# An attention output projection whose two operands are widened to float32r by casting DMAs

## The chip, the cores and the metric

The kernel runs on one core of a Trainium2 chip. The time is device microseconds of one execution; the median of 2 runs is shown. The profile is one execution, taken by the hardware profiler, and its times are microseconds from the first instruction.

## The reference

Two blocks follow each other on x of 2048 positions by 1024 features, in bfloat16. The first is a layer norm, a projection to q, k and v, a local attention of 32 heads of 32 features, and an output projection with `wo`. The second is a layer norm and a gated feed-forward network without an activation function.

```python
def attn(x, wqkv, wo):            # x: 2048 x 1024, H = 32 heads, Dh = 32
    q, k, v = split(x @ wqkv)
    # each position sees W = 8 keys, at distances 0, 2, 4 ... 14 behind it
    logits = einsum("bhsd,bhswd->bhsw", q, kg) * Dh ** -0.5   # masked before the start
    o = einsum("bhsw,bhswd->bhsd", softmax(logits), vg)
    return o @ wo                 # wo: 1024 x 1024
def ffn(x, w_gate, w_up, w_down): # F = 3584
    return ((x @ w_gate) * (x @ w_up)) @ w_down
h = x + attn(layernorm(x), wqkv, wo)
out = h + ffn(layernorm(h), w_gate, w_up, w_down)
```

## The kernel before

The 2048 positions are cut into four chunks of 512. For each chunk the work has these stages, all named by functions in the code.

- `ln1` loads x, normalises it on VectorE (DVE) and transposes it on TensorE (PE, line 111); ScalarE (ACT) copies the result to `lnT`.
- `qkv` multiplies by six blocks of `wqkv` of 512 columns each (`wq`, lines 134 and 144). All six are loaded once and stay for the four chunks. ACT copies each result out of PSUM to a tile `sg`, and SP writes it to tensors `qd`, `kd`, `vd` in device memory.
- `attention` reads these back in another layout, `qD`, `kD`, `vD`, by DMAs on the queue of POOL (GpSimd). There each of 128 partitions holds one head of one quarter of the chunk. Its arithmetic runs on DVE: products and sums for the logits (lines 177 to 183), softmax, then products and sums with v (lines 208 to 214) into `oD`. POOL writes `oD` to `od` in device memory, and reads it back by four DMAs as `oT` (line 218), the transposed layout that a matmul needs.
- `wo_ln2` is the output projection: two halves of 512 columns, and in each four tiles of 128 positions with 8 matmuls of 128x512 (line 234). DVE adds each result to x in `hs` (line 236). Then follow the second layer norm and its transposes.
- `ffn1` runs 7 blocks of gate and up weights (`wg`, `wu`, lines 251 and 255); ACT copies out of PSUM and DVE multiplies the two (line 261, `gs`).
- `ffn2` multiplies by `w_down` (line 290, in the last half of the last chunk line 277); DVE adds to `hs` (line 293), and SP stores the output.

Three things set the order. Each engine and each DMA queue runs its instructions in the order in which a scheduler placed them, after the priorities given by `prio`; the attention of the next chunk has a later place than the feed-forward work of the present chunk on PE, but runs beside it on DVE. Every wait is for data or for a buffer. And buffers come from pools: `wstream` has 6 buffers of 8 KB a partition, through which all weights go in turn, wqkv's six blocks first. `att` has one buffer for each tag, so a tile with the same tag as an earlier one waits until the last reader of that is done. PSUM has 6 buffers for matmul results (`mm`) and 2 for transposes; `t1k` has 31 buffers for `sg`, `gs` and `us`.

The projection of chunk 0 stands on PE between the two halves of `qkv` of chunk 3, that of a later chunk between `ffn1` and `ffn2` of the chunk before it.

Of the kernel before, what the change touches and what calls it, by code (L numbers as in the profile page):

```python
# [7 lines left out]

BF = mybir.dt.bfloat16
F32 = mybir.dt.float32  # L10
ALU = mybir.AluOpType
ACTF = mybir.ActivationFunctionType
PSUM = bass.MemoryType.PSUM
# [5 lines left out]
DH = 32  # L19
# [7 lines left out]
SUB = TC // 4  # L27
KO = D // 128
# [8 lines left out]
def kernel(  # L37
# [11 lines left out]
    nc = tc.nc  # L49
# [12 lines left out]
    wpool = ctx.enter_context(tc.tile_pool(name="wstream", bufs=6))  # L62
# [6 lines left out]
    att = ctx.enter_context(tc.tile_pool(name="att", bufs=1))  # L69
# [6 lines left out]
    make_identity(nc, ident[:])  # L76
    eps = const.tile([128, 1], F32)
    nc.vector.memset(eps[:], EPS)
    mask = const.tile([32, W, 16], F32)
    nc.vector.memset(mask[:], 0.0)  # L80
# [9 lines left out]
    wo_v = A_wo.rearrange("(kk p) n -> p kk n", p=128)  # L90
# [6 lines left out]
    def layernorm_T(src, dstT, col):  # L97
        st = small.tile([128, 2, nc.vector.BN_STATS_DIM], F32, tag="st")
        for i in range(2):
            nc.vector.bn_stats(out=st[:, i, :], in_=src[:, bass.ts(i, 512)])  # L100
        mv = small.tile([128, nc.vector.BN_AGGR_DIM], F32, tag="mv")
        nc.vector.bn_aggr(out=mv[:], in_=st[:])  # L102
        lnv = small.tile([128, 1], F32, tag="lnv")
        nc.scalar.activation(lnv[:], mv[:, 1:2], ACTF.Ln, bias=eps[:])  # L104
        rstd = small.tile([128, 1], F32, tag="rstd")
        nc.scalar.activation(rstd[:], lnv[:], ACTF.Exp, scale=-0.5)
        ln = lnp.tile([128, D], BF, tag="ln")
        nc.vector.tensor_scalar(ln[:], src[:], mv[:, 0:1], rstd[:], ALU.subtract, ALU.mult)  # L108
        pt = pstp.tile([128, KO, 128], BF, tag="pt")
        for kk in range(KO):  # L110
            nc.tensor.transpose(pt[:, kk, :], ln[:, bass.ts(kk, 128)], ident[:])  # L111
        nc.scalar.copy(dstT[:, :, col:col + 128], pt[:])  # L112
# [47 lines left out]
    def attention(c):  # L160
        qD = att.tile([128, DH, SUB], BF, tag="qD")
        kD = att.tile([128, DH, SUB + HB], BF, tag="kD")
        vD = att.tile([128, DH, SUB + HB], BF, tag="vD")
        nc.gpsimd.dma_start(qD[:], qd[c].rearrange("c g d s -> (c g) d s"))
        for (tD, td) in ((kD, kd), (vD, vd)):
            if c == 0:
                nc.gpsimd.dma_start(td[c][0, :, :, 0:HB], zt[:])
            else:
                nc.gpsimd.dma_start(td[c][0, :, :, 0:HB], td[c - 1][3, :, :, SUB:SUB + HB])
            nc.gpsimd.dma_start(tD[:], td[c].rearrange("c g d s -> (c g) d s"))  # L170
        lg = att.tile([128, W, SUB], F32, tag="lg")
        for wp in range(W // 2):
            prod = att.tile([128, 2, DH, SUB], BF, tag="prod")
            for j in range(2):
                w = 2 * wp + j
                o = HB - DIL * w
                nc.vector.tensor_tensor(prod[:, j], qD[:], kD[:, :, o:o + SUB], ALU.mult)  # L177
            nc.vector.tensor_tensor(prod[:, :, 0:16], prod[:, :, 0:16], prod[:, :, 16:32], ALU.add)  # L178
            nc.vector.tensor_tensor(prod[:, :, 0:8], prod[:, :, 0:8], prod[:, :, 8:16], ALU.add)
            t3 = att.tile([128, 2, 4, SUB], F32, tag="t3")  # L180
            nc.vector.tensor_tensor(t3[:], prod[:, :, 0:4], prod[:, :, 4:8], ALU.add)
            nc.vector.tensor_tensor(t3[:, :, 0:2], t3[:, :, 0:2], t3[:, :, 2:4], ALU.add)
            nc.vector.tensor_tensor(lg[:, 2 * wp:2 * wp + 2, :], t3[:, :, 0], t3[:, :, 1], ALU.add)
        if c == 0:
            nc.vector.tensor_tensor(lg[0:32, :, 0:16], lg[0:32, :, 0:16], mask[:], ALU.add)
        tr = att.tile([128, 4, SUB], F32, tag="t3")
        nc.vector.tensor_tensor(tr[:], lg[:, 0:4], lg[:, 4:8], ALU.max)
        nc.vector.tensor_tensor(tr[:, 0:2], tr[:, 0:2], tr[:, 2:4], ALU.max)
        mx = att.tile([128, SUB], F32, tag="mx")
        nc.vector.tensor_tensor(mx[:], tr[:, 0], tr[:, 1], ALU.max)  # L190
        nc.vector.tensor_tensor(lg[:], lg[:], mx[:, None, :].to_broadcast((128, W, SUB)), ALU.subtract)
        nc.scalar.activation(lg[:], lg[:], ACTF.Exp, scale=float(DH) ** -0.5)
        tr2 = att.tile([128, 4, SUB], F32, tag="t3")
        nc.vector.tensor_tensor(tr2[:], lg[:, 0:4], lg[:, 4:8], ALU.add)
        nc.vector.tensor_tensor(tr2[:, 0:2], tr2[:, 0:2], tr2[:, 2:4], ALU.add)
        sm = att.tile([128, SUB], F32, tag="mx")
        nc.vector.tensor_tensor(sm[:], tr2[:, 0], tr2[:, 1], ALU.add)
        rs = att.tile([128, SUB], F32, tag="rs")
        nc.vector.reciprocal(rs[:], sm[:])
        at = att.tile([128, W, SUB], BF, tag="at")  # L200
        nc.vector.tensor_tensor(at[:], lg[:], rs[:, None, :].to_broadcast((128, W, SUB)), ALU.mult)
        oD = att.tile([128, DH, SUB], BF, tag="oD")
        for wp in range(W // 2):
            pv = att.tile([128, 2, DH, SUB], BF, tag="prod")
            for j in range(2):
                w = 2 * wp + j
                o = HB - DIL * w
                nc.vector.tensor_tensor(pv[:, j], vD[:, :, o:o + SUB],  # L208
                                        at[:, w, None, :].to_broadcast((128, DH, SUB)), ALU.mult)
            if wp == 0:  # L210
                nc.vector.tensor_tensor(oD[:], pv[:, 0], pv[:, 1], ALU.add)
            else:
                nc.vector.tensor_tensor(pv[:, 0], pv[:, 0], pv[:, 1], ALU.add)  # L213
                nc.vector.tensor_tensor(oD[:], oD[:], pv[:, 0], ALU.add)  # L214
        nc.gpsimd.dma_start(od[c].rearrange("c g d s -> (c g) d s"), oD[:])
        oT = att.tile([128, KO, 4, SUB], BF, tag="oT")
        for cp in range(4):
            nc.gpsimd.dma_start(oT[:, :, cp, :], od[c][cp].rearrange("(hg hl) d s -> (hl d) hg s", hl=4))
        return oT

    def wo_ln2(c, oT):
        lnT = lnTp.tile([128, KO, TC], BF, tag="lnT")
        hs = []
        for t in range(4):
            ht = hp.tile([128, D], BF, tag="h")
            nc.sync.dma_start(ht[:], x[bass.ds(c * TC + t * 128, 128), :])
            hs.append(ht)
        for hf in range(2):
            wt = wpool.tile([128, KO, 512], BF, tag="w")
            nc.sync.dma_start(wt[:], wo_v[:, :, bass.ts(hf, 512)])  # L230
            for t in range(4):
                ps = psmm.tile([128, 512], F32, tag="mm")
                for kk in range(KO):
                    nc.tensor.matmul(ps[:], lhsT=oT[:, kk, t, :], rhs=wt[:, kk, :],  # L234
                                     start=(kk == 0), stop=(kk == KO - 1))
                nc.vector.tensor_tensor(hs[t][:, bass.ts(hf, 512)], ps[:], hs[t][:, bass.ts(hf, 512)], ALU.add)  # L236
        for t in range(4):
            layernorm_T(hs[t], lnT, t * 128)
        return lnT, hs
# [60 lines left out]
    for b in range(6):  # L300
        with prio(-9900 + 1000 * (b // 2) + b):
            wt = wpool.tile([128, KO, 512], BF, tag="w", name=f"wq{b}")
            nc.sync.dma_start(wt[:], wqkv_v[:, :, bass.ts(b, 512)])
            wq_sb.append(wt)
    for c in range(NCH):
        qkv(c, lnTs[c], B0)
        if c + 1 < NCH:
            with prio(-10000 + 1000 * (c + 1)):
                lnTs[c + 1] = ln1(c + 1)
        else:  # L310
            with prio(1000000):
                oT = attention(0)
            nxt = wo_ln2(0, oT)
        qkv(c, lnTs[c], B1)
    for c in range(NCH):
        lnT2, hs = nxt
        hT = ffn1(c, lnT2)
        if c + 1 < NCH:
            with prio(1000000 + (c + 1) * 20000):
                oT = attention(c + 1)  # L320
            nxt = wo_ln2(c + 1, oT)
        ffn2(c, hT, hs)
# [30 lines left out]
```

## Time and profile before

| what | value |
|---|---|
| median of the runs | 855.4 us (854.95 to 855.85) |
| span of the profiled execution | 853.2 us |
| PE busy | 827.4 us (97%), 4000 matmuls |
| PE weight loads busy | 383.4 us (45%) |
| DVE busy | 465.1 us (55%) |
| ACT busy | 234.6 us (27%) |
| POOL busy | 29.9 us (4%) |
| DMA | 151.65 MB, mean 178 GB/s |

The span goes from the first to the last instruction; what lies around it, 2.2 us to the median, is not in the profile. The profiled execution has no other time of its own than this span. Busy times of PE are those of pipelined matmuls: their lengths overlap, so that the distance between starts says more than the length of one. Lines such as L234 are lines of the kernel. "PEld" is TensorE's loading of weights, "SPq" and "POOLq" are the engines' queues as they issue DMAs.

### The profile page before, as it was taken

Reading aid. Unit: us, or ns where it says so; the run is one execution under the profiler, and the core shown is the slowest. Engines: PE = TensorE matmul, PEld = TensorE weight load, DVE = VectorE, ACT = ScalarE, POOL = GpSimd, SP = SyncE. Lnnn points to the kernel's source line nnn. Section 1 sums busy time; section 2 is a strip of 40 time slices with the busy share of each in tenths; the row PEclk is TensorE's granted clock in tenths of the full one; section 3 lists DMA queues with packets and bytes.
Section 4 is the critical chain, followed back from the end, with each engine's and each line's share of the span. In section 5 each row is a group of like instructions: output and inputs, shape, how many; then the busy total and the mean of one; then the engine's idle time right before and its main releaser. Section 6 shows DMA issues by size and latency. Waiting matters only on the chain.

```text
span 853.2 us, 9977 instructions
## 1 busy us (share of the span) xinstructions
PE 827.4 (97%) x4000; PEld 383.4 (45%) x4000; DVE 465.1 (55%) x523; ACT 234.6 (27%) x421; POOL 29.9 (4%) x46
## 2 busy tenths in 40 slices
PE   5999999969999997999999999999999999999998
PEld 4544444434444443444444444444444444444443
DVE  6719999998999999999931421111116102111011
ACT  4744333305333312003333120133332003333200
POOL 1000000200020000100000010000000000000000
PEclk9999999989999999999999999999999999999999
DMA  9896646975676743956455465653625465353520
GB/s 311 247 262 167 173 99 176 233 265 148 173 240 210 250 157 132 284 160 214 154 191 177 138 179 178 216 185 111 195 93 170 141 217 172 106 191 118 170 82 25
DMA packets 166798, 151.65 MB, mean 178 GB/s; under 512 B 55008, under 2 KB 159456, under 8 KB 164704
## 3 DMA queue, kind: packets, MB, share of 16 engines
q1 hardware_dynamic: 162912, 128.73, 50.3%
q0 software_dynamic: 3840, 22.28, 7.9%
q8 instruction: 31, 0.51, 0.2%
q14 instruction: 15, 0.12, 0.0%
HBM read 129.17 MB, written 22.02 MB: 177 GB/s over the span
## 4 chain that ended last, share of the span: by engine, by line
PE 68%; DVE 24%; ACT 3%; issue 2%; DMA 2%; SPq 0%; DVEq 0%; ACTq 0%
PE pu L255 21%; PE pg L251 21%; PE acc L290 16%; DVE prod L177 5%; DVE pv L208 4%; PE accl L277 3%; DVE prod L178 3%; PE ps L144 2%; PE ps L234 2%; DVE oD L214 2%; DVE st L100 2%; ACT lnT L112 1%; DVE pv L213 1%; DVE ln L108 1%; DVE ht L236 1%
## 5 line engine op out<-in xcount | busy, mean ns | idle before, releaser
L251 PE MATMUL pg<-lnT,wg 128*128 128x512 bf16 x896 | 211.7, 379 | 0.0
L255 PE MATMUL pu<-lnT,wu 128*128 128x512 bf16 x896 | 211.7, 379 | 0.0
L290 PE MATMUL acc<-wd,gs 128*128 128x512 bf16 x784 | 172.8, 381 | 3.1 <-DVE ht L236 2.3
L261 DVE TENSOR_TENSOR gs<-gs,us 128x512 bf16<-128x512 bf16 x112 | 47.2, 422 | 209.6 <-ACT us L260 209.6
L144 PE MATMUL ps<-lnT,wq 128*128 128x512 bf16 x736 | 161.3, 380 | 0.0
L258 ACT CAST gs<-pg 128x512 bf16<-128x512 f32 x112 | 65.7, 587 | 255.7 <-PE pg L251 254.6
L251 PEld LDWEIGHTS <-wg 128*128 128x128 bf16 x896 | 87.7, 98 | 105.7
L255 PEld LDWEIGHTS <-wu 128*128 128x128 bf16 x896 | 87.7, 98 | 105.7
L290 PEld LDWEIGHTS <-gs 128*128 128x128 bf16 x784 | 76.4, 98 | 94.8 <-issue 5.1
L144 PEld LDWEIGHTS <-wq 128*128 128x128 bf16 x736 | 71.9, 98 | 85.0 <-issue 0.8
L260 ACT CAST us<-pu 128x512 bf16<-128x512 f32 x112 | 65.7, 587 | 123.6 <-PE pu L255 122.4
L177 DVE TENSOR_TENSOR prod<-qD,kD 128x4096 bf16<-128x4096 bf16 x32 | 72.6, 2285 | 18.1 <-DMA kD<-kd 18.0
L147 ACT CAST sg<-ps 128x512 bf16<-128x512 f32 x96 | 55.8, 588 | 84.2 <-PE ps L144 79.1
L293 DVE TENSOR_TENSOR ht<-acc,ht 128x512 bf16<-128x512 f32 x28 | 17.4, 683 | 108.8 <-PE acc L290 108.8
L208 DVE TENSOR_TENSOR pv<-vD,at 128x4096 bf16<-128x4096 bf16 x32 | 72.4, 2286 | 0.3
L234 PE MATMUL ps<-wt,oT 128*128 128x512 bf16 x256 | 57.9, 387 | 3.4 <-DVE ht L236 3.4
L234 PEld LDWEIGHTS <-oT 128*128 128x128 bf16 x256 | 25.4, 99 | 35.3 <-issue 6.2
L178 DVE TENSOR_TENSOR prod<-prod 128x4096 bf16<-128x4096 bf16 x16 | 36.6, 2290 | 0.4
L111 PE MATMUL pt<-ident,ln 128*128 128x128 bf16 x256 | 21.3, 237 | 15.7 <-DVE ln L108 13.0
L112 ACT COPY lnT<-pt 128x1024 bf16<-128x1024 bf16 x32 | 31.1, 1012 | 10.2 <-PE pt L111 9.0
L104 ACT ACTIVATE lnv<-mv,eps 128x1 f32<-128x1 f32 x32 | 9.3, 295 | 80.2 <-DVE mv L102 80.1
L111 PEld LDWEIGHTS <-ln 128*128 128x128 bf16 x256 | 17.4, 106 | 24.4 <-DVE ln L108 22.1
(50 smaller groups left out, 330.0 us busy)
## 6 DMA issues: line engine op xcount, KB each, us to landing
wg<-in_B_w_gate_dram SPq DMA_DIRECT2D x28, 1024.0 KB, 5.3
wu<-in_B_w_up_dram SPq DMA_DIRECT2D x28, 1024.0 KB, 6.8
wd<-in_B_w_down_dram SPq DMA_DIRECT2D x32, 896.0 KB, 4.9
wt<-in_A_wo_dram SPq DMA_DIRECT2D x8, 1024.0 KB, 7.7
wq<-in_A_wqkv_dram SPq DMA_DIRECT2D x6, 1024.0 KB, 7.8
kD<-kd POOLq DMA_DIRECT2D x4, 1152.0 KB, 7.8
vD<-vd POOLq DMA_DIRECT2D x4, 1152.0 KB, 5.8
xt<-in_A_x_dram SPq DMA_DIRECT2D x16, 256.0 KB, 4.2
```

The costliest lines, as they stand in the source:

```text
L144: nc.tensor.matmul(ps[:], lhsT=wt[:, ko, bass.ts(j, 128)], rhs=lnT[:, ko, :], start=(ko == 0), stop=(ko == KO - 1))
L147: nc.scalar.copy(sg[:], ps[:])
L177: nc.vector.tensor_tensor(prod[:, j], qD[:], kD[:, :, o:o + SUB], ALU.mult)
L178: nc.vector.tensor_tensor(prod[:, :, 0:16], prod[:, :, 0:16], prod[:, :, 16:32], ALU.add)
L208: nc.vector.tensor_tensor(pv[:, j], vD[:, :, o:o + SUB], at[:, w, None, :].to_broadcast((128, DH, SUB)), ALU.mult)
L234: nc.tensor.matmul(ps[:], lhsT=oT[:, kk, t, :], rhs=wt[:, kk, :], start=(kk == 0), stop=(kk == KO - 1))
L251: nc.tensor.matmul(pg[:], lhsT=wg[:, ko, bass.ts(j, 128)], rhs=lnT[:, ko, :], start=(ko == 0), stop=(ko == KO - 1))
L255: nc.tensor.matmul(pu[:], lhsT=wu[:, ko, bass.ts(j, 128)], rhs=lnT[:, ko, :], start=(ko == 0), stop=(ko == KO - 1))
L258: nc.scalar.copy(gs[:], pg[:])
L260: nc.scalar.copy(us[:], pu[:])
L261: nc.vector.tensor_tensor(gs[:], gs[:], us[:], ALU.mult)
L290: nc.tensor.matmul(acc[t][:], lhsT=hT[f][:, bass.ts(t, 128)], rhs=wd[:, j, :], start=(f == 0), stop=(f == NF - 1))
```

## The change

Both operands of the output projection become float32r, a four-byte type. `oT` is allocated as float32r, so the four DMAs that read the bfloat16 `od` convert on their way. `wo` is loaded as float32r too: instead of one load of 8 x 512 columns for a half, on SP, there are two loads of 4 x 512 on POOL's queue, which convert as well. A tile of these has the size of a buffer of `wstream`, so that a half of `wo` takes two buffers instead of one. `oT` needs twice the space; for this `oD` gets the tag, and so the buffer, of `qD`.

```diff
-        oD = att.tile([128, DH, SUB], BF, tag="oD")
+        oD = att.tile([128, DH, SUB], BF, tag="qD")
...
-        oT = att.tile([128, KO, 4, SUB], BF, tag="oT")
+        oT = att.tile([128, KO, 4, SUB], F32R, tag="oT")
         for cp in range(4):
             nc.gpsimd.dma_start(oT[:, :, cp, :], od[c][cp].rearrange("(hg hl) d s -> (hl d) hg s", hl=4))
...
         for hf in range(2):
-            wt = wpool.tile([128, KO, 512], BF, tag="w")
-            nc.sync.dma_start(wt[:], wo_v[:, :, bass.ts(hf, 512)])
+            wts = []
+            for qh in range(2):
+                wt = wpool.tile([128, KO // 2, 512], F32R, tag="w", name=f"wo{qh}")
+                nc.gpsimd.dma_start(wt[:], wo_v[:, bass.ts(qh, KO // 2), bass.ts(hf, 512)])
+                wts.append(wt)
             for t in range(4):
                 ps = psmm.tile([128, 512], F32, tag="mm")
                 for kk in range(KO):
-                    nc.tensor.matmul(ps[:], lhsT=oT[:, kk, t, :], rhs=wt[:, kk, :],
+                    nc.tensor.matmul(ps[:], lhsT=oT[:, kk, t, :], rhs=wts[kk // 4][:, kk % 4, :],
                                      start=(kk == 0), stop=(kk == KO - 1))
```

In the order of the instructions that results, POOL issues for each chunk: `od`, four times `oT`, then loads of `wo` with the next chunk's `qD` among them (for chunk 0 behind the first load, for chunk 1 behind the second, for chunk 2 ahead of all four). Before, `qD` of the second chunk stood ahead of all these. In chunk 0 the fourth load of `wo` uses the buffer of the first.

## The prediction

> **What bounds the kernel now.** I read the 40 slices first, then the costliest groups, TensorE's waits, the timelines of PE and POOL around the output projection, and the DMA issues last.
>
> ```profile
> PE   5999999969999997999999999999999999999998
> ...
> DVE  6719999998999999999931421111116102111011
> ...
> PEclk9999999989999999999999999999999999999999
> ```
>
> PE is full throughout; the dents lie in slices 0, 8 and 15 (a slice is 21.3 us). DVE is as full up to about 430 us: until then the attention of all four chunks runs there, and what it delivers late, PE waits for.
>
> ```profile
> L234 PE MATMUL ps<-wt,oT 128*128 128x512 bf16 x256 | 57.9, 387 | 3.4 <-DVE ht L236 3.4
> L234 PEld LDWEIGHTS <-oT 128*128 128x128 bf16 x256 | 25.4, 99 | 35.3 <-issue 6.2
> ```
>
> These are the rows the change rewrites: 256 matmuls, each with its own weight load of 99 ns. Their lengths overlap, so spacing comes from the timeline (start us, us, engine, line, what):
>
> ```profile
> 149.73 16.78 PE L144 MATMUL ps<-lnT,wq 128*128 128x512 bf16 x77
> 166.35 10.52 PE L234 MATMUL ps<-wt,oT 128*128 128x512 bf16 x48
> 179.66 5.30 PE L234 MATMUL ps<-wt,oT 128*128 128x512 bf16 x16 [2.79 <-DVE ht L236]
> 184.80 2.10 PE L144 MATMUL ps<-lnT,wq 128*128 128x512 bf16 x9
> 190.80 1.89 PE L111 MATMUL pt<-ident,ln 128*128 128x128 bf16 x16 [3.90 <-DVE ln L108]
> ```
>
> In chunk 0 a burst of 48 takes 10.5 us. In chunk 2 all 64 run unbroken:
>
> ```profile
> 478.31 13.98 PE L234 MATMUL ps<-wt,oT 128*128 128x512 bf16 x64
> 492.12 1.10 PE L111 MATMUL pt<-ident,ln 128*128 128x128 bf16 x16
> ```
>
> From 478.31 to 492.12 is 13.81 us for 64, so 216 ns each; the 99 ns weight loads lie wholly under the stream. TensorE's waits over the whole span (total, times, longest):
>
> ```profile
> PE pt L111 <- DVE ln L108: 13.0, 6, 6.6
> PE ps L234 <- DVE ht L236: 3.4, 2, 2.8
> ```
>
> No wait for a DMA carries weight: the transfers are hidden. The POOL queue, with what ended each idle time:
>
> ```profile
> 95.49 0.53 POOL L164 DMA_DIRECT2D qD<-qd  x1 [24.92 <-DMA vd<-sg]
> ...
> 143.85 0.55 POOL L215 DMA_DIRECT2D od<-oD  x1 [3.33 <-DVE oD L214]
> 151.27 3.55 POOL L218 DMA_DIRECT2D oT<-od  x4 [6.87 <-DMA od<-oD]
> 154.81 0.79 POOL L169 DMA_DIRECT2D vd<-vd  x1
> ```
>
> The second chunk's qD is fetched at 95.5 us, during the first chunk's attention, so DVE goes from one attention into the next at 143.6 us without a gap. Sizes and times to landing:
>
> ```profile
> wt<-in_A_wo_dram SPq DMA_DIRECT2D x8, 1024.0 KB, 7.7
> ...
> qD<-qd POOLq DMA_DIRECT2D x4, 1024.0 KB, 5.4
> ...
> od<-oD POOLq DMA_DIRECT2D x4, 1024.0 KB, 6.7
> oT<-od POOLq DMA_DIRECT2D x16, 256.0 KB, 6.4
> ```
>
> **What the Trainium skill says.** "FP8 and Floating Point Precision", section TensorE Precision Notes: a reduced-precision form reads 4-byte values and truncates them, while true FP32 takes four passes through the array. "TensorE: Matmul & The Clock Gate", section Weight-path perf modes: the fast weight load needs 128 weights and a type that is not FP32; its section on LDWEIGHTS prices a plain load at columns / 1.2 ns, an estimated 107 ns for 128. "DMA: Bandwidth & Descriptors", section SWDGE vs HWDGE vs iDMA: a cast can only be issued from GpSimd, and all issuers share the same 16 engines. No float32r matmul and no cast is in the trace before, so it can confirm neither rate. Part 1 of the TensorE page says that an idle window halves the clock; here the trace agrees: the granted clock is 0.83 from 180 to 190 us and 0.72 from 190 to 196 us, round the 3.9 us gap.
>
> **The change part by part.**
>
> *The matmuls.* 256 stay 256, and in the changed program's instruction order they have no weight-load instruction of their own: each loads its weights itself. Lower bound: one pass and the load still under the stream, 216 ns, +0. Next: the estimated 107 ns load stands in front of each, 256 x 0.107 = +27 us. Half rate on 4-byte data: 256 x 0.216 = +55 us. Upper bound: four passes, 256 x 3 x 0.216 = +166 us. A gain is excluded: the stream of 512 columns stays. I take +0: the type is the reduced-precision one, and a 107 ns load fits under 216 ns as the 99 ns load does.
>
> *The weights of wo.* Before, 2 loads of 1024 KB a chunk on SP; now 4 of 512 KB source and 1024 KB destination on POOL, so 4 of the 6 buffers of the weight pool instead of 2, and twice the bytes written. For one load I take 8 us to landing (7.7 above); double (16 us) if the cast is slow. The SP queue loses 8 issues of 0.37 us, which nobody waited for.
>
> *oT* is written with twice the bytes. I take 8 us instead of 6.4.
>
> *oD in qD's buffer.* qD of the next chunk can start only once oD has been written to od, and in the changed POOL order it also stands behind oT x4 and the first wo load. Chunk by chunk:
>
> Chunk 0. oD is done at 143.85 and od has landed at 151.3 as before; oT is issued until 154.8, the first wo load (A) after it (its buffer, wq block 0, is free at 152.7, when wo was loaded before), then qD at about 156. A lands at 165, qD at about 166 to 169. The second load (B) waits for wq block 1, free at 161.5 (wo's second load before), and lands at 170 to 172. PE comes to the projection at 166.35 as before and stands still about 5 us until B. Half 0 is then done at 172 + 6.2 = 178. C (wq block 2, free at 166.3) has landed. D takes A's buffer, released at about 177, so it lands at about 185, while the 16 matmuls on C end at 182: 3 us more. The last 16 end at about 188.5 instead of 184.8. From there DVE sets the pace as before: two products (4.5 us), four evictions (0.68 each), statistics, ln. Before, PE spent 213.0 - 166.35 = 46.65 us here on 64 + 96 matmuls at 216 ns and 32 transposes at 59 ns (16 of them in 492.12 to 493.06) = 36.5 us: 10 us lost, clock included. Now I count 5 + 3 + 3 (ln) + 3 (clock) = 14. Net **+4 us** (-2 to +12; +35 with a slow cast, since oT, A, B and D then follow each other).
>
> Attention of chunk 1 starts at 169 instead of 143.6, 25 us late. DVE is full, so its oD comes at 241 + 25 = 266 and oT lands near 286. PE needs it at 309.5 + 4, so 27 us of slack hide the whole delay: **+0**.
>
> Chunk 2's qD stands behind A and B of chunk 1, which wait for the buffers of gate/up block 4, free near 213 + 5/7 x 96.5 = 282, plus 4. It lands near 293; attention 2 idles 27 us. Queued behind this first product on DVE are the gs multiplications, for which the second FFN stage waits; the changed order has eight of them ahead of it (8 x 3.45 us = 27 us of PE work), so they cover the gap. The projection of chunk 1 finds DVE in the middle of an attention as it did before: **+0** (-2 to +3).
>
> Attention 2 ends near 293 + 97 = 390; od, oT and qD follow in series (7 + 4 + 6), attention 3 runs from 407 to about 505 instead of 341 to 432. So the projection of chunk 2 (478 + 4) now meets a busy DVE. Before, from its start to the next steady stretch it lost 0.65 us (19.17 us elapsed for 77 matmuls and 32 transposes, 18.5); chunk 1, with attention beside it, lost 29.3 - 22.2 = 7.1 us. I take most of that difference: **+4 us** (0 to 6.5). Chunk 3's oT is ready near 525, its need is at 640: +0.
>
> Sum: 0 + 4 + 0 + 0 + 4 = +8 us on the profiled span of 853.2, so 861.2. The median of 855.4 stands 2.2 us above the span; I add that: 863.4, rounded to **863 us**.
>
> **The rivals.**
> *Weights in front of the stream* (slower). If the self-loaded 4-byte weights no longer hide, every one of the 256 matmuls pays 107 ns: 863 + 27 = 890; at half rate for 4-byte data 863 + 55 = 918. For it: no separate weight load is left to be pulled ahead, and the fast load is off. Against: 216 ns leave room for it. It decides from 16 us on the whole (a spacing of 216 + 36 = 252 ns makes 872, 2% over before).
> *Four passes*: 863 + 166 = 1029. Against it is only the type's name and the skill's distinction.
> *A slow cast*: landing times double, chunk 0 pays 35 instead of 4: 894. The later chunks have 27 us and more to hide it. For it: oT and A to D are all casts in one queue just where PE waits. Against: from 165 to 180 us the channels moved 255 GB/s beside all else, so bytes alone don't force it.
> *Less collision* (faster side): with attention 1 pushed back, DVE is free for evictions and ln at chunk 0, and the 10 us lost there come back in part, with no waits for B and D: 855 - 6 = 849; even with chunk 1's 7 us on top it stays within 2%. Against: the weight loads arrive later, not earlier.
>
> **How the numbers follow.** Forecast (850 to 872) 0.51; weights in front or half rate 0.22 (two thirds of it below 905); slow cast 0.13; four passes 0.10; less collision 0.04. The range reaches from 850 to 905 and leaves out the half rate and four passes, 0.17, and part of less collision. A measurement of this kernel tells about 2% from no change, 17 us: faster 0.01 (a part of less collision, if more comes back than I count), same 0.51 + 0.03 = 0.54, slower 0.22 + 0.13 + 0.10 = 0.45.
>
> **What would show it.** Right: in the group of the output projection a spacing of 216 to 225 ns in the last chunk's 64 matmuls (13.8 to 14.4 us in one burst); a new PE wait for the DMAs of wo in chunk 0 of 5 to 10 us; qD issues after oT in each chunk; a DVE gap of some 20 us before attention 1 and 2; PE as full as before elsewhere. Wrong: the burst of chunk 3 lasting 20 us or more (weights in front), 55 us (four passes); oT or wo landing after 12 us or more; a PE wait in chunk 1 or 3 for oT, which would mean that the slack of 27 us was gone.

## The result, and the profile after

The changed kernel takes 863.9 us (862.95 to 864.92), against 855.4 before: a ratio of 1.0098, 95% interval 1.0072 to 1.0125. The forecast was 863. The profiled execution has a span of 863.1 us against 853.2, so there are 9.9 us to explain, where the forecast counted 8; 1.8 us lie around the span (the time of that execution is 864.9). The sum came out close, but its terms did not; the rest of this text is about that.

The view of 40 slices, DVE and the granted clock:

```profile
DVE  6729996299994399994399993111116002111011
...
PEclk9999999999999999999999999999999999999999
```

DVE is no longer full without a break up to 430 us: it pauses in slices 6 and 7, 12 and 13, 18 and 19 (a slice is 21.6 us), ahead of attention 1, 2 and 3, whose `qD` comes late, and the attentions now end in slice 24, near 525 us instead of 430. The slices of the granted clock hide short drops, to which the text comes back. The groups of the output projection, and TensorE's waits over the span (total, times, longest):

```profile
L238 PE MATMUL ps<-wo,oT 128*128 128x512 f32 x256 | 63.9, 410 | 3.8 <-DMA wo<-in_A_wo_dram 3.8
...
L238 PEld LDWEIGHTS ps<-wo,oT 128*128 128x128 f32 x256 | 49.9, 196 | 16.7 <-DMA wo<-in_A_wo_dram 4.8
```

```profile
PE pt L112 <- DVE ln L109: 10.3, 6, 6.6
PE acc L294 <- DVE ht L240: 5.1, 4, 2.4
PE ps L238 <- DMA wo<-in_A_wo_dram: 3.8, 2, 3.5
PE pu L259 <- ACT us L264: 3.3, 1, 3.3
```

The weight loads do exist in the trace, 196 ns each instead of 99. The predicted wait for `wo` is there, but with 3.8 us below the 5 to 10 that were forecast. The wait of line 259 for ACT stood in no step of the prediction. The bursts of the projection in PE's timeline (start us, us, engine, line, what), first chunk 0, then chunk 3, where nothing disturbs it:

```profile
170.80 12.99 PE L238 MATMUL ps<-wo,oT 128*128 128x512 f32 x44 [3.46 <-DMA wo<-in_A_wo_dram]
...
184.84 3.98 PE L238 MATMUL ps<-wo,oT 128*128 128x512 f32 x16 [0.38 <-DMA wo<-in_A_wo_dram]
...
648.60 15.23 PE L238 MATMUL ps<-wo,oT 128*128 128x512 f32 x64
663.66 1.07 PE L112 MATMUL pt<-ident,ln 128*128 128x128 bf16 x16
```

From 648.60 to 663.66 is 15.06 us for 64 matmuls: 235 ns each, where the kernel before took 216. POOL's queue in chunk 0, and the DMA issues (times, KB each, median us to landing) with the line of POOL's own queue:

```profile
154.51 0.80 POOL L233 DMA_DIRECT2D wo<-in_A_wo_dram  x1
155.26 0.60 POOL L165 DMA_DIRECT2D qD<-qd  x1
```

```profile
q0 software_dynamic: 27648, 43.26, 21.7%
...
wo<-in_A_wo_dram POOLq DMA_DIRECT2D x16, 1024.0 KB, 6.3
oT<-od POOLq DMA_DIRECT2D x16, 512.0 KB, 7.5
...
qD<-qd POOLq DMA_DIRECT2D x4, 1024.0 KB, 12.8
```

The casts land as assumed, 6.3 and 7.5 us. Unforeseen is `qD`: 12.8 us instead of 5.4, issued right behind them (12.0, 13.7 and 15.5 us for chunks 1, 2 and 3). Half of the delay or more comes from the place in the queue and not from the casts: in the second experiment below `qD` stands behind plain loads of `oT`, and takes 10.2 to 10.5 us.

Where the 9.9 us went is read from PE's timeline, as the distance between the starts of stages. "WO" is the output projection and "F2" is FFN2, the work of `ffn2`, as FFN1 is that of `ffn1`. "WO 1 + F2 of chunk 0" is the projection of chunk 1 with the FFN2 of chunk 0, which follows it.

| stage | before | after | difference |
|---|---|---|---|
| start to FFN1 of chunk 0 (qkv, projection 0) | 212.8 | 210.9 | -1.9 |
| WO 1 + F2 of chunk 0 | 72.1 | 71.7 | -0.4 |
| FFN1 of chunk 1 | 96.7 | 101.2 | +4.5 |
| WO 2 + F2 of chunk 1 | 64.7 | 71.8 | +7.0 |
| WO 3 + F2 of chunk 2 | 64.7 | 65.9 | +1.1 |
| FFN1 of chunks 0, 2, 3 and the last F2 | 342.1 | 341.7 | -0.4 |

The slower rate (the larger spacing of the projection's matmuls) is 15.06 - 13.81 = 1.25 us a chunk, and is contained in four of these rows: 5.0 us together. The two stalls, both in chunk 1's feed-forward stages, where attention 3 now runs, are seen in these lines: ACT's timeline, then PE's.

```profile
460.50 0.58 ACT L262 CAST gs<-pg 128x512 bf16<-128x512 f32 x1 [1.14 <-PE pg L255]
472.50 1.06 ACT L193 ACTIVATE lg<-lg 128x1024 f32<-128x1024 f32 x1 [11.41 <-DVE lg L192]
```

```profile
474.08 3.16 PE L259 MATMUL pu<-lnT,wu 128*128 128x512 bf16 x8 [3.25 <-ACT us L264]
...
497.49 0.38 PE L294 MATMUL acc<-wd,gs 128*128 128x512 bf16 x1 [1.41 <-DVE ht L240]
500.29 0.38 PE L294 MATMUL acc<-wd,gs 128*128 128x512 bf16 x1 [2.42 <-DVE ht L240]
```

In the first pair ACT does nothing for 11.4 us. The Exp of attention 3 stands at the head of its queue and waits for the logits, which DVE has late because `qD` landed at 425 us; the casts that empty PSUM for FFN1 stand behind the Exp, and PE stops when PSUM is full. In the second block PE begins FFN2 and finds the PSUM buffers still held by the projection, since DVE is in the middle of an attention.

The stages lose more than these waits, since the granted clock drops with them: it is 0.50 from 473.3 to 476.7 us and again from 500.6 to 504.0, and the eight matmuls at 474.08 take 3.16 us where eight usually take 1.89. Half speed from 474.08 to 476.7 is an estimated 1.3 us, which with the wait of 3.25 makes up the 4.5 that FFN1 of chunk 1 lost.

### The profile page after: what moved, and what is told of

Same layout as the page of the kernel before. It is cut to its first block, busy times and chain, and to the rows that moved or that the text cites. A ratio compares the mean times of both kernels' runs of the same rounds, so it can differ in the third digit from the quotient of the medians.

```text
span 863.1 us, 9925 instructions
## 1 busy us (share of the span) xinstructions
PE 830.7 (96%) x3926; PEld 407.4 (47%) x4000; DVE 463.2 (54%) x523; ACT 233.8 (27%) x421; POOL 41.8 (5%) x62
## 3 DMA queue, kind: packets, MB, share of 16 engines
q0 software_dynamic: 27648, 43.26, 21.7%
## 4 chain that ended last, share of the span: by engine, by line
PE 61%; DVE 23%; DMA 6%; issue 5%; ACT 2%; POOL 2%; SPq 0%; DVEq 0%; POOLq 0%
PE acc L294 18%; PE pg L255 17%; PE pu L259 16%; DVE prod L178 5%; PE ps L145 4%; DMA qD<-qd 3%; DVE pv L209 3%; PE accl L281 3%; DVE prod L179 3%; PE ps L238 2%; DVE prod L180 1%; DVE t L182 1%; DVE st L101 1%; DVE ht L240 1%; ACT lnT L113 1%
## 5 line engine op out<-in xcount | busy, mean ns | idle before, releaser
L145 PE MATMUL ps<-lnT,wq 128*128 128x512 bf16 x718 | 159.2, 379 | 0.9
L209 DVE TENSOR_TENSOR pv<-vD,at 128x4096 bf16<-128x4096 bf16 x32 | 72.1, 2285 | 0.3
L238 PE MATMUL ps<-wo,oT 128*128 128x512 f32 x256 | 63.9, 410 | 3.8 <-DMA wo<-in_A_wo_dram 3.8
L238 PEld LDWEIGHTS ps<-wo,oT 128*128 128x128 f32 x256 | 49.9, 196 | 16.7 <-DMA wo<-in_A_wo_dram 4.8
L112 PE MATMUL pt<-ident,ln 128*128 128x128 bf16 x256 | 20.4, 231 | 12.7 <-DVE ln L109 10.3
L215 DVE TENSOR_TENSOR oD<-oD,pv 128x4096 bf16<-128x4096 bf16 x12 | 27.5, 2288 | 0.2
L214 DVE TENSOR_TENSOR pv<-pv 128x4096 bf16<-128x4096 bf16 x12 | 27.4, 2287 | 0.2
```

The lines of the kernel that those rows point to most:

```text
L145: nc.tensor.matmul(ps[:], lhsT=wt[:, ko, bass.ts(j, 128)], rhs=lnT[:, ko, :], start=(ko == 0), stop=(ko == KO - 1))
L209: nc.vector.tensor_tensor(pv[:, j], vD[:, :, o:o + SUB], at[:, w, None, :].to_broadcast((128, DH, SUB)), ALU.mult)
L238: nc.tensor.matmul(ps[:], lhsT=oT[:, kk, t, :], rhs=wts[kk // 4][:, kk % 4, :], start=(kk == 0), stop=(kk == KO - 1))
```

## The experiments

Two theories stood against each other after this. One says that the loss is the price of float32r itself: slower matmuls and heavier transfers. The other, called D below, says that most of it is an ordering effect: the shared buffer delays `qD`, and what the delay costs depends on what DVE's and ACT's in-order queues then have ahead of the instructions that empty PSUM. The expectations have further theories under other letters, each with its meaning beside it. Ratios are to the kernel before on the same chip, with 95% intervals; on the four chips used here that kernel took 855.4 to 856.7 us.

**The structure without the type.** Everything of the change, its queues, tags and number of loads, but in bfloat16 and so without a cast:

```diff
-        oT = att.tile([128, KO, 4, SUB], F32R, tag="oT")
+        oT2 = att.tile([128, 2, KO, 4, SUB], BF, tag="oT", name="oT")
+        oT = oT2[:, 0]
...
-                wt = wpool.tile([128, KO // 2, 512], F32R, tag="w", name=f"wo{qh}")
-                nc.gpsimd.dma_start(wt[:], wo_v[:, bass.ts(qh, KO // 2), bass.ts(hf, 512)])
+                wt = wpool.tile([128, KO, 512], BF, tag="w", name=f"wo{qh}")
+                nc.gpsimd.dma_start(wt[:, 0:KO // 2, :], wo_v[:, bass.ts(qh, KO // 2), bass.ts(hf, 512)])
```

> Everything of the changed kernel but the type: oT and wo stay bfloat16, in tiles as large as before (oT in half of its 16 KB, each half load of wo in one of the six weight buffers), wo still loaded in two parts on POOL, oD still in qD's buffer. Theory A (type and cast): 235 ns a matmul become 216 (-5 us), the oT transfers are cheap again, so that qD lands in 6 us instead of 12 to 15, attention 3 comes early enough, and the losses of the second feed-forward stage (4.5 us in its first half, some 3 of the 6.7 in its second) go: about 851 us. Theory B (buffers and queue): the placement carries the loss, only the 5 us of the matmuls go: about 859 us.

Measured: 870.2 us, 1.0186 (1.0162 to 1.021). Both forecasts were too low. It is slower than the float32r kernel by about 6 us, although its matmuls are the quicker ones, so the structure alone can cost more than the whole change. Where the changed kernel loses, this does not show: here projection 1 with FFN2 of chunk 0 takes 80.8 us (72.1 before, 71.7 in the changed kernel), and projection 2 with FFN2 of chunk 1 only 65.9.

**The shared buffer alone.** The kernel before, with one word changed:

```diff
-        oD = att.tile([128, DH, SUB], BF, tag="oD")
+        oD = att.tile([128, DH, SUB], BF, tag="qD")
```

> The kernel before with one edit: oD takes qD's buffer. Theory A: the late attention 1 helps chunk 0 (3 us) and chunk 1 (1.6 us), and attention 3 beside the projection of chunk 2 costs about 3: 853 to 854 us, within the noise of before. Theory B: the shared buffer alone delays attention until it costs what the changed kernel loses in chunk 2 (4.5 + 6.7 - 1.2 = 10 us) less the gain of chunks 0 and 1 (4.5): 861 us.

Measured: 872.1 us, 1.0197 (1.0182 to 1.0213). Both forecasts were too low here as well. The span grows by 15.7 us over before, 7.4 of them in projection 1 with FFN2 of chunk 0 (79.5 against 72.1), 4.3 up to FFN1 and 4.0 in FFN1 of chunk 1. PE's timeline in projection 1, then the last product of attention 2 and the first addition on DVE:

```profile
329.21 5.30 PE L234 MATMUL ps<-wt,oT 128*128 128x512 bf16 x16 [4.86 <-DVE ht L236]
340.14 1.03 PE L111 MATMUL pt<-ident,ln 128*128 128x128 bf16 x8 [5.64 <-DVE ln L108]
```

```profile
321.00 2.29 DVE L177 TENSOR_TENSOR prod<-qD,kD 128x4096 bf16<-128x4096 bf16 x1
...
328.47 0.68 DVE L236 TENSOR_TENSOR ht<-ps,ht 128x512 bf16<-128x512 f32 x1
```

The projection starts at 313.83 us, but in DVE's order all eight QK products of attention 2 stand ahead of the first addition out of PSUM, which comes at 328.47, 14.6 us later. In the changed kernel only four products stand ahead of it, and it comes 8.7 us after the projection's start (316.07 against 307.41). DVE's lines of the changed kernel:

```profile
308.60 2.29 DVE L178 TENSOR_TENSOR prod<-qD,kD 128x4096 bf16<-128x4096 bf16 x1
...
316.07 0.68 DVE L240 TENSOR_TENSOR ht<-ps,ht 128x512 bf16<-128x512 f32 x1
```

In both kernels attention 2 begins late because of the shared buffer, in this one even earlier (at 285.25 us) than in the changed one (294.98). What differs is the order in which DVE then does the products and the additions.

**The type alone.** The changed kernel with `oD` in a buffer of its own again; the space comes from a third buffer of `lnT`:

```diff
-    lnTp = ctx.enter_context(tc.tile_pool(name="lnT", bufs=3))
+    lnTp = ctx.enter_context(tc.tile_pool(name="lnT", bufs=2))
...
-        oD = att.tile([128, DH, SUB], BF, tag="qD")
+        oD = att.tile([128, DH, SUB], BF, tag="oD")
```

> The changed kernel with a buffer of its own for oD (8 KB, taken from the third buffer of lnT). qD can be fetched early again, with all casts kept. Theory A: the losses of chunk 2 (10 us) go, the gains of chunks 0 and 1 (4.5) go as well, the 5 us of the matmuls stay: 858 to 861 us. Theory C (the casts themselves, in every chunk, whatever the attention does): no change, 863 to 864 us.

Measured: 860.5 us, 1.0069 (1.0053 to 1.0086). FFN1 of chunk 1 is back at 96.5 us and projection 2 with its FFN2 at 66.1, so both stalls are gone. In their place chunk 0 takes 215.8 us instead of 210.9, with PE waiting 7.5 us for `wo` instead of 3.8.

**Its control.** The kernel before with the same two buffers of `lnT`:

```diff
-    lnTp = ctx.enter_context(tc.tile_pool(name="lnT", bufs=3))
+    lnTp = ctx.enter_context(tc.tile_pool(name="lnT", bufs=2))
```

> The kernel before with two instead of three buffers for lnT, the price of the space in the run with a buffer of its own for oD. All theories: two are alive at once at most, so 855 us within 2; if it is more than 2 us off, that difference is taken off that run.

Measured: 854.4 us, 0.999 (0.9981 to 0.9999). The third buffer is worth nothing. Against this control, the type with its casts and loads costs 860.5 - 854.4 = 6.1 us, of which the rate is 5.0. So D does not hold for the total: without the shared buffer about two thirds of the loss stay. In the changed kernel the two stalls cost 4.5 + 5.8 = 10.3 us, but what chunks 0 and 1 gained, 4.8, pays back almost half of that, and the net price of the shared buffer is about 3 us (863.9 - 860.5).

**What sets the rate.** The changed kernel with each float32r matmul cut into two of 256 columns:

```diff
-                for kk in range(KO):
-                    nc.tensor.matmul(ps[:], lhsT=oT[:, kk, t, :], rhs=wts[kk // 4][:, kk % 4, :],
-                                     start=(kk == 0), stop=(kk == KO - 1))
+                for nh in range(2):
+                    for kk in range(KO):
+                        nc.tensor.matmul(ps[:, bass.ts(nh, 256)], lhsT=oT[:, kk, t, :],
+                                         rhs=wts[kk // 4][:, kk % 4, bass.ts(nh, 256)],
+                                         start=(kk == 0), stop=(kk == KO - 1))
```

> The changed kernel with every float32r matmul of the projection cut into two of 256 columns, each with its own weight load: 512 matmuls and loads instead of 256. Read in the last burst (chunk 3, 128 matmuls), which nothing disturbs. If each self-loaded weight leaves a fixed 20 ns uncovered: 108 + 20 = 128 ns each, 16.3 us for the burst instead of 15.06. If the stream itself is 9% slower for 4-byte data: 118 ns, 15.1 us as before. If the load is what bounds (188 ns in the trace, hidden only by a stream of 216): 188 ns or more, 24 us and more for the burst, and some 36 us on the whole.

Measured: 870.2 us, 1.0157 (1.0135 to 1.0179). Chunk 3's burst in PE's timeline:

```profile
653.25 15.71 PE L239 MATMUL ps<-wo,oT 128*128 128x256 f32 x128
668.80 1.07 PE L112 MATMUL pt<-ident,ln 128*128 128x128 bf16 x16
```

15.55 us for 128 matmuls is 121 ns each. A weight load takes 189 ns here in the median, so it cannot be what spaces them: then 128 would take 24 us. Two halves cost 243 ns where the whole costs 235; the cost follows the columns, with a few ns for each instruction. Why the columns of float32r pass more slowly than the 216 ns of bfloat16, no run here shows. The burst is only 0.5 us longer than with 512 columns, so most of the 6 us that this kernel loses over the changed one is not the rate: it has other waits, 7.6 us for `wo` and 13.3 for `ln`, with other instructions ahead of others. That part was not taken further.

**Moving the attention away from the projection.** The changed kernel, with `qD` of chunks 2 and 3 placed in `oT`'s buffer, so that attention starts only after the projection that reads `oT` (this edit is called the gate below):

```diff
-        qD = att.tile([128, DH, SUB], BF, tag="qD")
+        qD = att.tile([128, DH, SUB], BF, tag="qD" if c < 2 else "oT", name="qD")
```

> The changed kernel with qD of chunks 2 and 3 in oT's buffer, so that these attentions cannot start before the projection of the chunk before has read its oT. Theory D (what costs is attention work that stands in DVE's queue ahead of the projection's evictions and the gs multiplications, and comes late): the projections of chunks 1 and 2 then find DVE free, as chunk 3's does; 5 us go in chunk 1, 4.5 and 5.5 in chunk 2: about 849 us. Theory A in its first form (the late qD and the casts cost by themselves): attention is later still, so not faster than 863.

Measured: 864.0 us, 1.0087 (1.0061 to 1.0114), no gain, where D had forecast about 849. Projections 1 and 2 run without a wait and FFN1 of chunk 1 is at 96.5 us, but FFN2 of chunks 0 and 1 takes 57.8 and 58.0 us instead of the 50 that it takes undisturbed. PE at the boundary between FFN2's halves:

```profile
353.66 26.05 PE L294 MATMUL acc<-wd,gs 128*128 128x512 bf16 x108 [5.18 <-DVE ht L297]
```

The stall has moved: now it is FFN2's four accumulators whose additions to `hs` stand behind five products on DVE.

**The same in the kernel before.** The same line changed there:

```diff
-        qD = att.tile([128, DH, SUB], BF, tag="qD")
+        qD = att.tile([128, DH, SUB], BF, tag="qD" if c < 2 else "oT", name="qD")
```

> The same gate in the kernel before, all in bfloat16, oD in its own buffer. Theory D: the 7 us that the projection of chunk 1 loses beside attention 2 go, and nothing comes back in chunk 2: about 847 to 849 us. Theory A: the attention of chunks 2 and 3 starts some 80 us later, and as there is slack before its oT is needed, no change: 855.

Measured: 858.3 us, 1.0017 (1.0009 to 1.0025). D's number, 847 to 849, missed again. The wait is at the same place (PE waits 6.8 us there for DVE's additions), so it does not come from the type.

**`qD` on another queue.** The changed kernel with that load issued by SP:

```diff
-        nc.gpsimd.dma_start(qD[:], qd[c].rearrange("c g d s -> (c g) d s"))
+        nc.sync.dma_start(qD[:], qd[c].rearrange("c g d s -> (c g) d s"))
```

> The changed kernel with qD loaded on SP instead of POOL, so that it does not queue behind the casting oT transfers in POOL's ring. It should land in about 6 us instead of 12 to 15. Theory A: the gaps on DVE ahead of attention 1 and 3 shrink by 6 to 10 us, the first half of the loss in chunk 2 (4.5 us) goes: 857 to 860. Theory D: the order on DVE puts all eight products of attention 2 ahead of the evictions of chunk 1, as with the shared buffer alone, which costs up to 8 us more there: 862 to 868.

Measured: 874.7 us, 1.0211 (1.0173 to 1.025), slower than both forecasts. Attention 3 does start earlier (at 395.6 us instead of 425), and FFN1 of chunk 1 with projection 2 and its FFN2 becomes 9.0 us shorter than in the changed kernel. But SP's queue holds the first `qD` up as well: attention 0 starts at 71.0 us instead of 59.6, the stages up to FFN1 take 223.0 us instead of 210.9, and projection 1 with FFN2 of chunk 0 takes 4.5 more. As a remedy it fails; that an earlier `qD` takes most of the loss of chunk 1 away, it shows.

**Taking DVE off PSUM.** If D is right about the queues, the gate pays as soon as the PSUM of FFN2 is emptied by an engine that has no products in its queue. The kernel before, with the gate, two buffers of `lnT`, and

```diff
+    accp = ctx.enter_context(tc.tile_pool(name="accp", bufs=4))
...
-                nc.vector.tensor_tensor(hs[t][:, bass.ts(hf, 512)], acc[t][:], hs[t][:, bass.ts(hf, 512)], ALU.add)
+                ac = accp.tile([128, 512], F32, tag="ac")
+                nc.scalar.copy(ac[:], acc[t][:])
+                nc.vector.tensor_tensor(hs[t][:, bass.ts(hf, 512)], ac[:], hs[t][:, bass.ts(hf, 512)], ALU.add)
```

> The kernel before, with qD of chunks 2 and 3 in oT's buffer (so that attention c starts only after projection c-1), and with the FFN2 accumulators copied out of PSUM by ScalarE to a float32 tile before DVE adds them to hs (not in the last half of the last chunk). Theory D (a buffer's price is what DVE's in-order queue then has ahead of a PSUM eviction): the earlier gate run moved 5 us of waiting from the projection to FFN2's half boundary, where DVE had attention products ahead of the four additions; with ScalarE emptying PSUM there, that wait goes too. WO of chunk 1 14.8 us, FFN2 of chunk 0 50 to 51 us instead of 57.5 (before) and 55.3 (gate alone), so 847 to 850 us, ratio 0.991 to 0.995. Theory R (DVE is simply overloaded: the work of attention beside the feed-forward stages costs the same 7 us wherever it stands): FFN2 or FFN1 of the next chunk pays it, 854 to 858 us, ratio 1.00.

Measured: 851.1 us, 0.9943 (0.9928 to 0.9958). Projection 1 is at 14.75 us and FFN2 of chunk 0 at 49.99, as D expected: 7.4 us less than before. But FFN1 of chunks 1 and 2 grew by 1.8 each, for a new wait of PE for ACT's copies, so half of that gain came back elsewhere, as theory R (DVE is overloaded) would have it.

**The copy without the gate.** The kernel before with two buffers of `lnT` and only

```diff
+    accp = ctx.enter_context(tc.tile_pool(name="accp", bufs=4))
...
-                nc.vector.tensor_tensor(hs[t][:, bass.ts(hf, 512)], acc[t][:], hs[t][:, bass.ts(hf, 512)], ALU.add)
+                ac = accp.tile([128, 512], F32, tag="ac")
+                nc.scalar.copy(ac[:], acc[t][:])
+                nc.vector.tensor_tensor(hs[t][:, bass.ts(hf, 512)], ac[:], hs[t][:, bass.ts(hf, 512)], ALU.add)
```

> The kernel before, with the copy by ScalarE out of the FFN2 accumulators, without the gate. Theory D: the waits of projection 1 for DVE's evictions (2.8 us) and the later ones for ln stay, only the wait at FFN2's half boundary goes: 852 to 855 us, ratio 0.996 to 1.000. Theory R: the same as before, or slower by ScalarE's 16 to 28 more copies, 855 to 858 us.

Measured: 854.5 us, 0.9981 (0.9974 to 0.9989), as the control with two `lnT` buffers. By itself the copy brings nothing; it needs the attention moved.

**Both edits in the float32r kernel.** The changed kernel with two buffers of `lnT`, and

```diff
+    accp = ctx.enter_context(tc.tile_pool(name="accp", bufs=4))
...
+        qD = att.tile([128, DH, SUB], BF, tag="qD" if c < 2 else "oT", name="qD")
...
+                ac = accp.tile([128, 512], F32, tag="ac")
+                nc.scalar.copy(ac[:], acc[t][:])
+                nc.vector.tensor_tensor(hs[t][:, bass.ts(hf, 512)], ac[:], hs[t][:, bass.ts(hf, 512)], ALU.add)
```

> The changed kernel with both edits of the first of these runs (gate, and ScalarE's copy out of the FFN2 accumulators). Theory D: the stall in FFN1 of chunk 1 (4.5 us), that of projection 2 with FFN2 after it (6.5 us), and FFN2 of chunk 0's 7 us go; what is left of the change is the rate of the float32r matmuls, 4 x 1.2 us, and chunk 0: 846 to 853 us, 3 to 6 us more than the bfloat16 kernel with the same two edits. Theory R: the 7 us stay in each of FFN2 of chunk 0 and 1, as when only the gate was set: 860 to 864 us.

Measured: 861.0 us, 1.0053 (1.0034 to 1.0071). The total lies where R put it, but not for R's reason: FFN2 of chunks 0 and 1 is at 49.9 us, but FFN1 of chunks 1 and 2 at 103.4 and 101.7. ACT's timeline where FFN1 of chunk 1 begins, and PE's:

```profile
380.59 1.06 ACT L194 ACTIVATE lg<-lg 128x1024 f32<-128x1024 f32 x1 [28.68 <-DVE lg L193]
381.56 2.03 ACT L299 COPY ac<-acc 128x512 f32<-128x512 f32 x4
```

```profile
382.17 3.57 PE L256 MATMUL pg<-lnT,wg 128*128 128x512 bf16 x8 [4.05 <-ACT ac L299]
```

It is the stall of the changed kernel once more: an Exp at the head of ACT's queue, ready only when DVE is, and behind it the copies that PE needs.

**The Exp behind the copies.** The same kernel; the Exp of attention 2 and 3 gets a bias of zero made from FFN1's fourth `gs`, which puts it later on ACT (`hT` is the list of these `gs`, handed to `attention` as a new argument):

```diff
-        nc.scalar.activation(lg[:], lg[:], ACTF.Exp, scale=float(DH) ** -0.5)
+        if c < 2:
+            nc.scalar.activation(lg[:], lg[:], ACTF.Exp, scale=float(DH) ** -0.5)
+        else:
+            zb = small.tile([128, 1], F32, tag="zb")
+            nc.scalar.activation(zb[:], hT[3][:, 0:1], ACTF.Copy, scale=0.0)
+            nc.scalar.activation(lg[:], lg[:], ACTF.Exp, scale=float(DH) ** -0.5, bias=zb[:])
```

> The previous float32r kernel (gate, and ScalarE's copy out of the FFN2 accumulators), with one thing more: the Exp of attention 2 and 3 takes a bias of zero that is made from the fourth gs of FFN1, so that on ScalarE's queue it stands behind the four accumulator copies and the first eight casts of FFN1 instead of ahead of them. Theory D (what stalls PE in FFN1 is an Exp at the head of ScalarE's in-order queue that waits for the logits from DVE): FFN1 of chunks 1 and 2 goes from 103.4 and 101.7 us back to 96.5, the rest stays, so 848 to 851 us, ratio 0.990 to 0.994; the float32r kernel then costs over the bfloat16 one only its rate. Theory R (DVE is behind with its work, and the Exp is only where it shows): the FFN1 stages stay above 100 us, or the 12 us turn up in the projections and FFN2 after them, 858 to 862 us.

Measured: 847.95 us, 0.990 (0.9882 to 0.9918). ACT's timeline at the same place:

```profile
372.84 2.05 ACT L304 COPY ac<-acc 128x512 f32<-128x512 f32 x4 [22.15 <-PE acc L300]
...
388.61 1.15 ACT L199 ACTIVATE lg<-lg,zb 128x1024 f32<-128x1024 f32 x1
```

The copies now start as soon as PE has written, and all FFN1 stages are at 96.5 to 96.7 us, all FFN2 stages undisturbed. DVE was not too slow for its work: the 12 us that FFN1 of chunks 1 and 2 lost did not come back anywhere. On ACT only the two Exps (one in each attention) changed their places, with the new copies that make the bias ahead of them; on DVE the steps that need the Exp moved back with it, behind some of the multiplications for `gs`. With float32r operands and all, this kernel is 13 us faster than the one without this edit, 16 us faster than the change, and 1% faster than the kernel before. A bfloat16 kernel with all three edits was not run.

## Why the prediction was right, and where it was not

*The total* was right to 1 us, and that was luck in good part. On the span it forecast +8 us and +9.9 came: the rate, FFN1 of chunk 1 and projection 2 were taken 11.3 us too low, chunks 0 and 1 8.8 us too high. By the steps:

- *The matmuls*, taken at +0: the step that failed. Measured +1.25 us a chunk, 5.0 in all. The choice between one pass and four was right: 235 ns is far from 864, as the Trainium skill's distinction in "FP8 and Floating Point Precision" (TensorE Precision Notes) would have it. The argument "a 107 ns load fits under 216 ns" used the estimate from "TensorE: Matmul & The Clock Gate", section LDWEIGHTS; the measured load takes 188 ns in the median and 196 in the mean. It still hides (256-column matmuls at 121 ns exclude that it stands in front), but the spacing is 9% longer for a reason that the load does not give.
- *Chunk 0*, taken at +4: the wrong sign. The waits that it named were there, with 3.5 us for B and 0.4 for D instead of 5 and 3. But the stages up to FFN1 became 1.9 us shorter, or 3.2 without the rate. The rival "less collision" was right here in its main point: attention 1 is held back to 167.3 us, DVE makes its first addition at 175.29 and takes the others between single products, and two waits of PE for DVE are gone, the 2.8 us inside this projection and the 3.9 us ahead of the transposes after it.
- *Attention 1*, +0 for 25 us of delay: right. DVE paused 23.9 us, and no stage of PE shows it.
- *Chunk 1*, +0: close (-0.4 with the rate), and in part luck. `qD` of chunk 2 was put at 293 us, and the first product ran at 294.98, but by two errors: it was issued at 281.20 instead of about 287, and took 13.7 us to land instead of about 6. Experiments 1 and 2 show that the +0 was not safe: with the shared buffer alone this place costs 7.4 us, when DVE's order is another one. In this kernel's order only four products stand ahead of the first addition.
- *Chunk 2's projection beside attention 3*, taken at +4 (0 to 6.5): right in mechanism. WO 2 + F2 lost 7.0, 1.25 of them rate, so 5.8.
- *What no step had*: FFN1 of chunk 1, +4.5. The prediction let attention 3 start at 407, with `qD` landing 6 us after issue. It was issued at 409.45, since attention 2 ended later than assumed, and landed at 425, 15.5 us after that, behind the loads of `oT` on POOL's queue. The Exp, which waited for DVE, then blocked ACT for 11.4 us. The Trainium skill says it in "PSUM — Partial Sum Buffer", section Engine vs sequencer instructions: ScalarE's and VectorE's queues are strictly first in, first out. The trace agrees: no cast passed the Exp from 461.1 to 472.5 us. The prediction looked at what stands behind a late DVE instruction on DVE, not at what stands behind the Exp on ACT. That this Exp is the cause in the changed kernel itself is read from its trace; moving it was tried in the kernel with both other edits, where 12 us went.
- *The slow cast* as a rival was wrong: 6.3 and 7.5 us to landing. What the casts add appears in the next transfer on the queue, `qD`: 12.0 to 15.5 us behind casts of `oT` against 10.2 to 10.5 behind plain loads of it in experiment 2, so an estimated 1.4 to 5.3 us by these two runs. The rest of its delay is the place in the queue.

Sum of what was measured: rate 5.0, FFN1 of chunk 1 4.5, projection 2 5.8, chunk 0 -3.2, chunk 1 -1.6, the remainder -0.6: 9.9 us.

Not settled: whether the 9% of the rate belong to the type or to the chip's state as well. In the last experiment, on another chip, the three undisturbed bursts take 14.7 us, 230 ns each, and in every other float32r run with 512 columns 15.1. The granted clock doesn't explain it: it is 1.00 in the bursts of chunk 3 of both kernels. Nor is it known what the changed kernel gains when only its Exps are moved.

## What to carry to other kernels

A buffer that is shared to make room has no price of its own: the same tag cost 17 us in the bfloat16 kernel and about 3 us in the float32r one, depending on what the in-order queues had ahead of the instructions that empty PSUM. So for every load that a change makes later, follow its consumer through all the engines it uses, and ask on each what is queued behind it and who waits for that. An instruction that waits for a late engine should stand behind the instructions that empty PSUM on its own queue: here, in the kernel with the two other edits, putting two Exps there gained 13 us, where the type with its casts and loads cost 6.1. And a forecast of the total that comes true proves nothing of its terms.

## What the runs showed of the hardware

- Float32r matmuls of 128x512 run at 235 ns each against 216 in bfloat16, those of 128x256 at 121. Their weight loads take 196 ns in the mean against 99, and don't set the spacing: at 256 columns the matmuls follow each other faster than one load lasts.
- POOL's queue moved 27648 packets instead of 3840. In the trace's records a casting load of `oT` goes in packets of 512 B at 74 ns each, where the plain one had 4096 B at 254 ns, so 6.9 bytes (as written, four to an element) per ns of an engine instead of 16.1. Yet a cast of `oT` landed only 1.1 us later than the plain load (7.5 against 6.4).
- A plain load of 1024 KB issued behind the casts of `oT` on the same queue took 12.0 to 15.5 us to land, behind plain loads of `oT` 10.2 to 10.5, and with neither ahead of it 5.2 to 5.6.
